# Batch 0's head loads on SyncE, its folds in quarters, and an earlier softmax in a cross-covariance attention with FFN kernel

## Chip, cores and metric

One core of a Trainium2 chip. The metric is the device time of one execution in microseconds (us), smaller is better. The span of a profiled execution is about 2 us shorter than its time.

## The reference

```python
def _attn_ref(q, k, v, tau):                       # B, N, C = 4, 5824, 256
    qn = q / (norm(q, axis=1) + 1e-6)
    kn = k / (norm(k, axis=1) + 1e-6)
    s = kn.transpose(0, 2, 1) @ qn / tau           # 256 x 256 per batch
    a = exp(s - s.max(-1)); a /= a.sum(-1) + 1e-9
    return v @ a

def _moe_ref(x, w1, w2, w3, w_out):                # x: 23296 x 256, d_ff 1024
    return ((x @ w1) * (x @ w2)) @ w3 @ w_out
```

## The kernel before

The kernel folds each batch's 256x256 attention matrix into the weights w1 and w2 (`Wf`), and w3 with w_out into one matrix (`W_sb`). Then the main loop needs only v, transposed: 11 chunks of 512 rows and a short one per batch, and per chunk eight steps `j`, each with two products `a`, `b` (2 matmuls of 512 columns each), one multiplication and up to two groups of output matmuls `o`. While batch b runs in this loop, the scores of batch b+1 (`G`, from q and k) and its softmax and folds are put in between, at set values of a clock that counts the planned TensorE time from the first `a` of the batch. I call the place where the softmax and folds of the next batch meet the end of this one a joint; there are three.

What the argument needs:

```python
    load_piece("k", 0, 0, (half,))      # GpSimd, f32 -> bf16 in the transfer
    load_piece("q", 0, 0, (half,))
    ...
        def first_folds():              # batch 0, before the first `a`
            sum_mm(0)
            fold_mm(0, 0)
            fold_mm(1, 0)
            sum_mm(1)
            fold_mm(0, 1)
            fold_mm(1, 1)
            fold(2)
            transpose_half_on_pe(0, 0, 0, False)
            fold(3, on_act=True)
            fold(4, "out", on_act=False)
            fold(5, "out")
    ...
            + [(0.2, 15.5, sums)]                                             # batches 1 to 3
            + [(0.43, 16.5 + 0.85 * i, lambda i=i: fold(i)) for i in range(8)]
    ...
    def hold(src):                      # GpSimd stands until src has been written
        nc.gpsimd.tensor_copy(gate_t, src)
    ...
        if b == 0:
            for i in range(2):
                at(1.5 + 0.6 * i, 0.43, soft0[5 + i])
            ...
            moves = [("v", 0, 3, 29.0), ("qk", 1, 0, 38.0), ("qk", 1, 1, 43.0), ("v", 0, 4, 50.0), ("qk", 1, 2, 58.0)]
            moves += [("qk", 1, 3, 63.0), ("v", 0, 5, 70.0), ("qk", 1, 4, 81.0), ("qk", 1, 5, 87.0)]
            moves += [("v", 1, 0, 96.0), ("v", 1, 1, 106.0), ("v", 1, 2, 116.0), ("qk", 2, 0, 126.0)]
            t0, t1 = 57.0, 115.5        # the scores of batch 1 are spread over this clock time
        ...
        before = (0, 2) if b == 0 else None
        for nm, m, pi, t in moves:
            if before is not None:      # the load that follows a load of v waits for v's DMA transpose
                at(t, 0.0, lambda w=before: hold(...vTs of piece w...))
            at(t, 0.0, gate)
            if nm == "qk":
                at(t, 0.0, lambda m=m, pi=pi: load_qk(m, pi))
                before = None
            else:
                at(t, 0.0, lambda m=m, pi=pi: load_piece("v", m, pi))
                at(t + 4.0, 0.0, lambda m=m, pi=pi: transpose_piece(m, pi))   # SyncE, DMA transpose
                before = (m, pi)
```

Each name in `moves` stands for a load of one piece (8 of 45 row tiles). All loads go out from GpSimd, one after the other, so a `hold` stops every load behind it. `gate` is of the same kind: it lets GpSimd stand until the loop's latest product has been made, so that a load goes out no sooner than its place on the clock.

## Time and profile before

| | before |
|---|---|
| time, median (six runs beside the changed kernel) | 573.24 us (572.98 to 575.30) |
| span of the profiled execution | 571.7 us |
| TensorE busy | 559.4 us, 98% |
| first `a` of the main loop | 40.69 us |
| chain that ended last | TensorE 92%, DMA 5% |

TensorE is the bound: before 40.69 us it waits for q and k of batch 0, after it it hardly rests. The lines stand in the prediction. To see small losses I kept one account for every run: for a stretch of the trace, the time from the first matmul start in it to the first start after it, less the matmuls in between, each with N/2400 + 0.0026 us for N columns (0.216 us at 512 and 0.109 at 256, the two rates that the steady stretch shows). What is left is TensorE time lost to waits and to a lower clock. Single matmul records are missing from some traces; each missing record of a fold reads as 0.22 us of loss and is taken off. By it the kernel before loses 1.02, 0.67 and 1.55 us at its three joints (168 to 192, 290 to 320, 424 to 454 us), 0.77 in the last chunk, and under 0.1 us in any stretch between them. The expectations of the experiments were written with a coarser count, up to 0.4 us off; the numbers in the text are the exact ones.

### The profile page before, as it was taken

The page shows a single profiled execution, that of the slowest core. Times are in us where ns is not written, and L with a number is a line of the kernel's source. Part 1 is how long each engine was busy: PE and PEld are TensorE (multiplying, and loading weights), DVE is VectorE, ACT ScalarE, POOL GpSimd, SP SyncE. Part 2 cuts the span into 40 slices and gives each one's busy share as a digit, 9 for nine tenths or more (in the row PEclk, how much of TensorE's full clock was granted, in tenths as well). Part 3 has the DMA queues.
Part 4 walks back from the last instruction along what each step waited for, and adds up shares of the span by engine and source line. Part 5 has one row for each costly group of instructions (what it writes and reads, how often), then busy time and mean ns, then how long its engine had stood idle before and what let it go on. Part 6 is the DMA issues. An engine that isn't in the chain of part 4 may idle for free.

```text
span 571.7 us, 10102 instructions
## 1 busy us (share of the span) xinstructions
PE 559.4 (98%) x3750; PEld 354.5 (62%) x3750; DVE 377.4 (66%) x612; ACT 337.7 (59%) x624; POOL 83.3 (15%) x164
## 2 busy tenths in 40 slices
PE   7789999999999999999999999999999999999997
PEld 4655576776666666666666666666665666666665
DVE  1047744788977567887776667778876656565564
ACT  0046644777856567776766567767766554454453
POOL 5250020303030111121030012031120000000000
PEclk9999999999999999999999999999999999999999
DMA  8999959869685697495661595665640325221011
GB/s 163 211 187 208 184 104 240 170 149 242 140 183 118 123 204 150 94 192 121 145 144 72 99 215 123 140 136 126 175 110 38 85 73 148 63 63 75 38 72 58
DMA packets 74560, 76.93 MB, mean 135 GB/s; under 512 B 54160, under 2 KB 58256, under 8 KB 74512
## 3 DMA queue, kind: packets, MB, share of 16 engines
q0 software_dynamic: 15504, 39.46, 39.3%
q1 hardware_dynamic: 58784, 36.64, 22.2%
q8 instruction: 29, 0.48, 0.3%
q10 hardware_dynamic: 224, 0.20, 0.1%
q14 instruction: 19, 0.16, 0.1%
HBM read 78.91 MB, written 23.86 MB: 180 GB/s over the span
## 4 chain that ended last, share of the span: by engine, by line
PE 92%; DMA 5%; DVE 1%; ACT 1%; POOL 1%; issue 0%; ACTq 0%; POOLq 0%
PE o L479 28%; PE a L438 27%; PE b L438 27%; PE G L188 5%; DMA k<-in_k_dram 5%; PE fold L349 2%; PE w L596 1%; ACT as L444 0%; ACT kr L279 0%; POOL k L109 0%; POOL q L109 0%; DVE abs L453 0%; PE sqk L221 0%; DVE vT L136 0%; DVE abs L455 0%
## 5 line engine op out<-in xcount | busy, mean ns | idle before, releaser
L453 DVE TENSOR_TENSOR abs<-as,b 128x512 bf16<-128x512 bf16 x336 | 230.5, 687 | 141.4 <-ACT as L444 130.3
L444 ACT CAST as<-a 128x512 bf16<-128x512 f32 (+1 forms) x384 | 216.1, 563 | 176.9 <-DVE abs L453 90.2
L438 PEld LDWEIGHTS <-Wf 128*128 128x128 bf16 x1536 | 149.2, 98 | 102.0 <-issue 1.9
L479 PE MATMUL o<-W_sb,abs 128*128 128x256 bf16 x1376 | 209.6, 273 | 0.1
L438 PE MATMUL a<-vT,Wf 128*128 128x512 bf16 x704 | 209.4, 379 | 0.2
L438 PE MATMUL b<-vT,Wf 128*128 128x512 bf16 x704 | 209.3, 379 | 0.0
L479 PEld LDWEIGHTS <-abs 128*128 128x128 bf16 x1376 | 134.5, 98 | 81.6 <-DVE abs L455 0.3
L197 DVE TENSOR_TENSOR acc<-acc,sq 128x1024 f32<-128x1024 f32 x66 | 80.4, 1219 | 0.4 <-ACT sq L185 0.3
L188 PE MATMUL G<-k,q 128*128 128x256 bf16 x276 | 49.9, 273 | 0.0
L185 ACT ACTIVATE sq<-q 128x512 f32<-128x512 bf16 x66 | 41.8, 634 | 0.0
L185 ACT ACTIVATE sq<-k 128x512 f32<-128x512 bf16 x66 | 41.6, 630 | 0.0
L426 POOL COPY gate_t<-abs 1x1 bf16<-1x1 bf16 x39 | 13.9, 355 | 167.7 <-DVE abs L453 167.0
L500 DVE COPY osb<-o 128x512 f32<-128x512 f32 x44 | 30.1, 685 | 0.7 <-PE o L479 0.7
L430 POOL COPY gate_t<-vT 1x1 bf16<-1x1 bf16 x17 | 4.4, 258 | 169.3 <-DMA vT<-v 134.0
L188 PEld LDWEIGHTS <-q 128*128 128x128 bf16 x276 | 27.0, 98 | 3.1
L499 ACT COPY osb<-o 128x512 f32<-128x512 f32 x44 | 25.8, 586 | 3.8 <-PE o L479 1.8
L279 ACT ACTIVATE kr<-row 128x256 f32<-128x256 f32 x1 | 0.4, 385 | 31.6 <-PE row L267 31.6
L109 POOL DMA_DIRECT2D q<-in_q_dram x29 | 15.7, 541 | 13.2 <-DMA k<-in_k_dram 6.0
L349 PE MATMUL fold<-w,e 128*128 128x512 bf16 x64 | 17.0, 380 | 0.5 <-DVE vT L136 0.4
L356 ACT ACTIVATE Wf<-fold,rs 128x512 bf16<-128x512 f32 x16 | 10.9, 688 | 8.1 <-PE fold L349 6.4
L244 DVE TENSOR_TENSOR dk<-sqk,ident 128x256 f32<-128x256 f32 x1 | 0.4, 425 | 21.3 <-PE sqk L221 21.3
L109 POOL DMA_DIRECT2D k<-in_k_dram x25 | 13.8, 551 | 3.7 <-DMA k<-in_k_dram 1.9
(89 smaller groups left out, 240.4 us busy)
## 6 DMA issues: line engine op xcount, KB each, us to landing
out_dram<-osb SPq DMA_DIRECT2D x44, 512.0 KB, 3.1
k<-in_k_dram POOLq DMA_DIRECT2D x19, 512.0 KB, 8.5
v<-in_v_dram POOLq DMA_DIRECT2D x19, 512.0 KB, 5.2
q<-in_q_dram POOLq DMA_DIRECT2D x18, 512.0 KB, 6.6
w_wout<-in_moe_w_dram POOLq DMA_DIRECT2D x1, 2048.0 KB, 23.6
k<-in_k_dram POOLq DMA_DIRECT2D x4, 320.0 KB, 9.9
v<-in_v_dram POOLq DMA_DIRECT2D x4, 320.0 KB, 5.4
q<-in_q_dram POOLq DMA_DIRECT2D x4, 256.0 KB, 12.0
```

The costliest lines, as they stand in the source:

```text
L109: nc.gpsimd.dma_start(out=pieces[nm, n, pi][:, lo:hi, :], in_=qk_main[nm, n][0][:, pi * PIECE + lo : pi * PIECE + hi, :])
L185: nc.scalar.activation(out=dst[:, :, part, :], in_=src[:, o : o + 2, :], func=AF.Square)
L188: nc.tensor.matmul(G[:, ct, :], lhsT=qt[:, i, ct * P : (ct + 1) * P], rhs=kt[:, i, :], start=(pr == 0 and part == 0 and ct == 0), stop=(pr ...
L197: nc.vector.tensor_add(accs[n], accs[n], sqs[0])
L349: nc.tensor.matmul(st["fold", i], lhsT=st["e"][:, c2, c1 * P : (c1 + 1) * P], rhs=w12[:, c2, w, h * 512 : (h + 1) * 512], start=(c2 == 0), ...
L426: nc.gpsimd.tensor_copy(gate_t, last_ab[0][:1, :1])
L438: nc.tensor.matmul(t[:, :n], lhsT=Wf[b][:, ct, w, j * P : (j + 1) * P], rhs=rhs_of(b, c, ct), start=(ct == 0), stop=(ct == CT - 1),)
L444: nc.scalar.copy(a_sb[:, :n], tiles[0][:, :n])
L453: nc.vector.tensor_mul(ab, a_sb, tiles[1])
L479: nc.tensor.matmul(tl[h][:, o, :], lhsT=lhsT, rhs=W_sb[:, j, :], start=(j == 0 and o == 0), stop=(j == FT - 1 and (small or o == 1)), skip ...
L499: nc.scalar.copy(o[:, 0:2, :], tl[0])
L500: nc.vector.tensor_copy(o[:, 2:4, :], tl[1])
```

## The change

The intent is in four parts. (1) The first halves of q and k of batch 0 come from SyncE in f32, sooner than GpSimd starts, and are cast. (2) Only the first quarter of the folded weights is made before the first `a`, the rest after it. (3) In batch 0, q and k of batch 1 are loaded ahead of late pieces of v, and the scores of batch 1 start at clock 46, not 57. (4) The later softmaxes start up to 4 us sooner, and every other fold goes to the bank `G` of the products. The core of the diff:

```diff
         def first_folds():
             sum_mm(0)
-            fold_mm(0, 0)
-            fold_mm(1, 0)
+            for c1 in range(CT):
+                quarter_mm(0, c1, 0)
             sum_mm(1)
-            fold_mm(0, 1)
-            fold_mm(1, 1)
-            fold(2)
-            transpose_half_on_pe(0, 0, 0, False)
-            ...
+            for c1 in range(CT):
+                quarter_mm(0, c1, 1)
+        def second_quarter():
+            ...
-            + [(0.2, 15.5, sums)]
-            + [(0.43, 16.5 + 0.85 * i, lambda i=i: fold(i)) for i in range(8)]
+            + [(0.2, 16.5, sums)]
+            + [(0.43, 17.8 + 0.9 * i, lambda i=i: fold(i, "G" if i % 2 else "ab")) for i in range(8)]
...
-    load_piece("k", 0, 0, (half,))
-    load_piece("q", 0, 0, (half,))
+    for nm in "kq":
+        new_piece(nm, 0, 0)
+        raw[nm] = work.tile([P, half, C], F32, tag="o_sb", name=f"raw_{nm}", bufs=3)
+        nc.sync.dma_start(out=raw[nm], in_=qk_main[nm, 0][0][:, :half, :])
+        load_part(nm, 0, 0, half, PIECE)
...
+    nc.vector.tensor_copy(pieces["k", 0, 0][:, :half, :], raw["k"])
+    nc.scalar.copy(pieces["q", 0, 0][:, :half, :], raw["q"])
...
-    for h in range(2):            # w1, w2 by halves of 512 columns
+    for f0, f1 in ((0, 256), (256, 512), (512, F)):
...
-            for i in range(2):
-                at(1.5 + 0.6 * i, 0.43, soft0[5 + i])
+            at(0.5, 0.87, soft0[5])
+            for i in range(4):
+                at(2.3 + 0.6 * i, 0.43, soft0[6 + i])
...
-            moves = [("v", 0, 3, 29.0), ("qk", 1, 0, 38.0), ("qk", 1, 1, 43.0), ("v", 0, 4, 50.0), ("qk", 1, 2, 58.0)]
-            moves += [("qk", 1, 3, 63.0), ("v", 0, 5, 70.0), ("qk", 1, 4, 81.0), ("qk", 1, 5, 87.0)]
-            moves += [("v", 1, 0, 96.0), ("v", 1, 1, 106.0), ("v", 1, 2, 116.0), ("qk", 2, 0, 126.0)]
-            t0, t1 = 57.0, 115.5
+            moves = [("qk", 1, 0, 29.0), ("v", 0, 3, 30.0), ("qk", 1, 1, 43.0), ("qk", 1, 2, 47.0), ("v", 0, 4, 53.0)]
+            moves += [("qk", 1, 3, 62.0), ("qk", 1, 4, 66.0), ("v", 0, 5, 72.0), ("qk", 1, 5, 81.0)]
+            moves += [("v", 1, 0, 94.0), ("v", 1, 1, 104.0), ("v", 1, 2, 114.0), ("qk", 2, 0, 126.0)]
+            t0, t1 = 46.0, 104.0
         else:
             ...
-            t0, t1 = 16.0, 104.0
+            t0, t1 = 16.0, 99.0
```

More of the change, by code (lines that the diff above doesn't have):

```diff
@@ L340, in sums, with fold_mm @@
             sum_mm(1)
-        def fold_mm(i, c2, tag="ab", on_act=None):
-            h, rest = divmod(i, 4)
-            w, c1 = divmod(rest, 2)
+        def fold_mm(key, c2, tag="ab", on_act=True):
+            w, c1, lo, hi = key
             if c2 == 0:
-                st["fold", i] = psum.tile(
-                    [P, 512], F32, tag=tag, name=f"fold_{n}_{i}", bufs={"ab": 4, "out": 3}[tag]
+                st[key] = psum.tile(
+                    [P, 512], F32, tag=tag, name=f"fold_{n}_{w}_{c1}_{lo}", bufs={"ab": 4, "out": 3, "G": 1}[tag]
                 )
+            m = st[key][:, : hi - lo]
             nc.tensor.matmul(
-                st["fold", i], lhsT=st["e"][:, c2, c1 * P : (c1 + 1) * P], rhs=w12[:, c2, w, h * 512 : (h + 1) * 512],
+                m, lhsT=st["e"][:, c2, c1 * P : (c1 + 1) * P], rhs=w12[:, c2, w, lo:hi],
                 start=(c2 == 0), stop=(c2 == CT - 1),
@@ L353, in fold_mm @@
             if c2 == CT - 1:
-                dst = Wf[n][:, c1, w, h * 512 : (h + 1) * 512]
-                if on_act if on_act is not None else i % 2 == 0:
-                    nc.scalar.activation(out=dst, in_=st["fold", i], func=AF.Copy, scale=st["rs"][:, c1 : c1 + 1])
-                else:
-                    nc.vector.tensor_scalar_mul(dst, st["fold", i], st["rs"][:, c1 : c1 + 1])
-        def fold(i, tag="ab", on_act=None):
-            fold_mm(i, 0, tag)
-            fold_mm(i, 1, tag, i % 2 == 0 if on_act is None else on_act)
+                dst = Wf[n][:, c1, w, lo:hi]
@@ new lines, in fold_mm, with fold, quarter_mm @@
+                if on_act:
+                    nc.scalar.activation(out=dst, in_=m, func=AF.Copy, scale=st["rs"][:, c1 : c1 + 1])
+                else:
+                    nc.vector.tensor_scalar_mul(dst, m, st["rs"][:, c1 : c1 + 1])
+        def fold(i, tag="ab"):
+            h, rest = divmod(i, 4)
+            w, c1 = divmod(rest, 2)
+            for c2 in range(CT):
+                fold_mm((w, c1, h * 512, (h + 1) * 512), c2, tag, i % 2 == 0)
+        def quarter_mm(lo, c1, c2):
+            if c2 == 0:
+                tag = "ab" if lo == 0 else "out"
+                st[lo, c1] = psum.tile(
+                    [P, 2, 256], F32, tag=tag, name=f"quarter_{lo}_{c1}", bufs={"ab": 4, "out": 3}[tag]
+                )
+            m = st[lo, c1]
+            for w in range(2):
+                nc.tensor.matmul(
+                    m[:, w, :], lhsT=st["e"][:, c2, c1 * P : (c1 + 1) * P], rhs=w12[:, c2, w, lo : lo + 256],
+                    start=(c2 == 0 and w == 0), stop=(c2 == CT - 1 and w == 1), skip_group_check=True,
+                )
+            if c2 == CT - 1:
+                for o in (0, P) if lo == 0 else (slice(0, 256),):
+                    cols = slice(o, o + P) if lo == 0 else o
+                    dst, src = Wf[n][:, c1, :, lo : lo + 256][:, :, cols], m[:, :, cols]
+                    if c1 == 0:
+                        nc.scalar.activation(out=dst, in_=src, func=AF.Copy, scale=st["rs"][:, c1 : c1 + 1])
+                    else:
+                        nc.vector.tensor_scalar_mul(dst, src, st["rs"][:, c1 : c1 + 1])
@@ L364, in first_folds @@
         def first_folds():
             sum_mm(0)
-            fold_mm(0, 0)
-            fold_mm(1, 0)
+            for c1 in range(CT):
+                quarter_mm(0, c1, 0)
             sum_mm(1)
-            fold_mm(0, 1)
-            fold_mm(1, 1)
-            fold(2)
-            transpose_half_on_pe(0, 0, 0, False)
-            fold(3, on_act=True)
-            fold(4, "out", on_act=False)
-            fold(5, "out")
+            for c1 in range(CT):
+                quarter_mm(0, c1, 1)
@@ L377, in soft_units @@
+        def second_quarter():
+            for c1 in range(CT):
+                for c2 in range(CT):
+                    quarter_mm(256, c1, c2)
         if n == 0:
-            return [k_first, k_row, q_first, scaled_first, first_folds] + [lambda i=i: fold(i) for i in range(6, 8)]
+            return [k_first, k_row, q_first, scaled_first, first_folds, second_quarter] + [lambda i=i: fold(i) for i in range(4, 8)]
         return (
@@ L511 @@
     half = PIECE // 2
-    busy(14)
-    load_piece("k", 0, 0, (half,))
-    load_piece("q", 0, 0, (half,))
+    busy(10)
+    raw = {}
+    for nm in "kq":
[3 more added lines that the diff above has]
+        load_part(nm, 0, 0, half, PIECE)
     w3_wout = vT_pool.tile([P, (NT - 1) * C], BF16, tag="vT", name="w3_wout")
@@ L561 @@
     load_piece("q", 0, 5, (1, 3, 4))
-    for h in range(2):
-        hs = slice(h * F // 2, (h + 1) * F // 2)
-        nc.gpsimd.dma_start(out=w12[:, :, 0, hs], in_=w1r[:, :, hs])
-        nc.gpsimd.dma_start(out=w12[:, :, 1, hs], in_=w2r[:, :, hs])
-        if h == 0:
-            new_piece("v", 0, 0)
-        load_part("v", 0, 0, h * half, (h + 1) * half)
+    new_piece("v", 0, 0)
+    load_part("v", 0, 0, 0, half)
+    for f0, f1 in ((0, 256), (256, 512), (512, F)):
+        nc.gpsimd.dma_start(out=w12[:, :, 0, f0:f1], in_=w1r[:, :, f0:f1])
+        nc.gpsimd.dma_start(out=w12[:, :, 1, f0:f1], in_=w2r[:, :, f0:f1])
+    load_part("v", 0, 0, half, PIECE)
     load_piece("v", 0, 1)
@@ L588 @@
     soft0[3]()
-    busy(4)
+    busy(3)
+    transpose_half_on_pe(0, 0, 0, False)
     soft0[4]()
```

## The prediction

> **What bounds the kernel now.** I read the page first, then the chain of waits, then the timeline from 0 to 82 us, then busy time in short windows at the start and at the three places where one batch's softmax meets the next batch.
>
> From the page, its first part and its share of the chain that ended last:
>
> ```profile
> PE 559.4 (98%) x3750; PEld 354.5 (62%) x3750; DVE 377.4 (66%) x612; ACT 337.7 (59%) x624; POOL 83.3 (15%) x164
> PE 92%; DMA 5%; DVE 1%; ACT 1%; POOL 1%; issue 0%; ACTq 0%; POOLq 0%
> ```
>
> TensorE is the bound, and DMA has 5% of the chain. In the chain in order of time that share is two pieces at the start:
>
> ```profile
> 4.52 11.89 DMA k<-in_k_dram
> 16.69 14.79 DMA k<-in_k_dram
> 31.53 0.84 PE sqk L221 x12
> ...
> 39.07 0.70 DVE vT L136
> 39.82 1.04 PE fold L349 x4
> 40.85 0.43 PE a L438 x2
> ```
>
> Columns are start, length, what. Until 31.5 us the kernel waits for k and q of batch 0; then come softmax and folding, and the first product `a` of the main loop. The timeline has that product's start at 40.69. From there until 567.72 (end of the last matmul) TensorE hardly rests. To see how hardly, I counted matmuls by shape. In the ab-only stretch (57.57 to 63.62) seven steps of four 512-column matmuls take 6.05 us, so 0.216 us each, and a 256-column one 0.109 (four with L479 fill the 1.300 us step: (1.300-0.864)/4). By these rates the matmuls after 40.69 need about 523.3 us, of 527.0. Some 3.7 us are lost: about 0.9 around 168-190 us, 0.5 around 296-318, 1.5 around 428-450, 0.8 in the last chunk. The last is untouched by the change. So the whole change plays for the 40.7 us before the loop and for under 3 us inside it.
>
> The very start, windows of 0.5 us (length; then PE, PEld, DVE, ACT, POOL busy; clock, DMA share, GB/s):
>
> ```profile
> 2.00:2.50 0.50, 0.50 (x3) 0.16 (x2) 0.00 (x0) 0.01 (x1) 0.50 (x2) 1.00 0.00 0
> 2.50:3.00 0.50, 0.50 (x3) 0.22 (x2) 0.00 (x0) 0.00 (x0) 0.50 (x2) 1.00 1.13 53
> 3.00:3.50 0.50, 0.50 (x3) 0.22 (x2) 0.00 (x0) 0.00 (x0) 0.50 (x2) 1.00 0.49 66
> 3.50:4.00 0.50, 0.50 (x3) 0.15 (x1) 0.00 (x0) 0.00 (x0) 0.50 (x3) 1.00 1.00 184
> 4.00:4.50 0.50, 0.50 (x2) 0.15 (x1) 0.00 (x0) 0.00 (x0) 0.50 (x2) 1.00 1.16 209
> ```
>
> The DMA engines do nothing before 2.5 us, full rate comes at about 3.5, and from there to 31 us they run at 205 to 225 GB/s (counted on the bf16 side) without a gap. That stream is the bound of the head, so what starts it sooner ends it sooner.
>
> **What the Trainium skill says.** "DMA: Bandwidth & Descriptors", section "Latency and other measured facts", gives a first byte after about 0.6 us for DMAs issued from SyncE or ScalarE and about 1 us for those of GpSimd. The trace has GpSimd's first issue at 1.22 and the first DMA activity at 2.5, so 1.3 us here; no SyncE load stands in it to compare. The same page, "Queues, rings and completion order", says that each DMA engine takes turns between the queues that have work: so SyncE's two loads will share the engines with GpSimd's from 2.5 us on, and the total is what counts. "TensorE: Matmul & The Clock Gate", section "Back-to-back issue gap", gives N/2.4 + 2.5 ns for an isolated warm matmul, 215.8 ns at 512 columns; the trace agrees (216). "PSUM — Partial Sum Buffer", section "Specifications (TRN2)", counts 8 banks; the kernel's pools take 4 (ab), 3 (out) and 1 (G), all 8, which is why folds can only borrow.
>
> **The change part by part.**
>
> *First halves of q and k by SyncE in f32, then cast.* No bytes of HBM are saved; the stream starts sooner. SyncE is released as the other engines are (the first DVE work is at 0.80). I take its issue at 0.8 to 1.0 and data at full rate from about 2.4 instead of 3.5; in 2.5 to 3.5 the engines moved only 60 of 209 GB/s, so part of that hole is filled. Estimate 1.0 us, between 0.5 and 1.5. The casts (128x1024) are new: 0.7 to 1.2 us on DVE by what its 1024-element copies and adds take (687, 1219 ns), 1.0 on ACT (the 128x1024 copy of vT took 1.01). Both engines are idle then (ACT until 33.6), and the first squares, now at 6.24 us, do not set the end: TensorE waits again for pieces at 11, 14 and 20 us. Four warm-up matmuls fewer cost and save nothing. After 24.8 us TensorE waited only 0.4 us, but its work is released by these landings, so it moves with them.
>
> *Quarters first.* Before, between the exponentials (37.37) and 40.69 stand 10 of 12 fold matmuls, a transpose of v with its 0.70 us evacuation, and a wait for w; the timeline shows both gaps:
>
> ```profile
> 38.87 0.59 PE L349 MATMUL fold<-w,e 128*128 128x512 bf16 x2
> 39.82 1.04 PE L349 MATMUL fold<-w,e 128*128 128x512 bf16 x4 [0.35 <-DVE vT L136]
> 40.69 0.59 PE L438 MATMUL a<-vT,Wf 128*128 128x512 bf16 x2
> ```
>
> After, only eight 256-column matmuls (0.87 us) come first, four before the last exponential lands; they end near 38.05. The row sums' reciprocal is ready near 38.1 as now, then one 256-element evacuation on ACT and DVE each (0.42, from 0.40 for such shapes and 0.69 to 0.75 for 512). First `a` near 38.75: 1.94 us sooner. But more is owed after it: before, two folds (0.87 us); now the second quarter (0.87) and four folds (1.73), 2.60 in all. Net 1.94 - 1.73 = 0.2 us. TensorE idles about 0.7 us there for the evacuation, where it idled about 0.9. The transpose moves into the idle time before the exponentials; its v is now loaded ahead of the weights and should land near 34.6 (w's first load did, issued at 30.0 and 4.6 us later), before TensorE reaches it at about 35.7.
>
> *Order of loads in batch 0 and earlier scores.* Same bytes, same matmuls. Scores of batch 1 move from clock 57-115 to 46-104, into the stretch in which output matmuls are caught up, where a step has 1.73 us of TensorE for one DVE multiplication. It removes the meeting of folds with the short last chunk (around 175-182).
>
> *Later softmax sooner, folds by turns in G.* The same 16 matmuls per batch. By the instruction order, all folds now end before chunk 11; previously they ran into it in all three batches. Two of three folds in a group no longer take ab banks together. Against it: in each batch two folds in the single G bank follow with only one other fold (0.43 us) between them, and need an evacuation of 0.75 on DVE: up to 0.5 us of stall. The exponentials' ping-pong (ACT waits 1.09 us for DVE, four times in batches 2 and 3) stays. Of about 2.9 us lost at these places I expect 0.5 back, between -0.5 and 1.5.
>
> Sum: 1.0 + 0.2 + 0.5 = 1.7 us, so 571.4. As each part shifts work that had slack rather than adding any, I lean a little further: 571.2.
>
> **Rivals.**
> 1. *The DMA start gives nothing*: two f32 writes of 0.5 MB share the engines and cost more than bf16 ones, or the quarters' 512-byte rows slow the weights (single-token loads around 31 to 33 us went at 135 to 153 GB/s). For it: DMA share is already above 1. Against: all reads are f32 anyway. Then only 0.7 us remain: 572.4.
> 2. *A wait for W's own transposes takes its place.* The w3T transposes are issued at 59.85, when w3 has landed, take 4.4 us, and were needed at 67.07: a slack of 2.8 us. The need comes 1.94 us sooner relative to the DMA stream, so about 0.9 remains. A slower weight load would use it up: at worst 1 us, 572.2.
> 3. *Early scores wait for q and k.* Piece 1 of batch 1 waits for v3's transpose; I get its landing near 92 and its need near 94. If late, TensorE stops for 1 to 3 us: up to 574.
> 4. *The full prize*: the stream starts 1.5 us sooner and the batch joints lose only half of what they did: 1.5 + 0.2 + 1.5, 569.9.
>
> **Range and chances.** The parts' spread gives 569.3 to 572.9. 2% is 11.5 us. Faster by that would need more than all idle time inside the loop plus a head shortened by a fifth: 1 in 100. Slower by that would need a stall that no view suggests.
>
> **What would show it.** DMA activity before 2.5 us and the last k landing near 30.5 show step one; first `a` near 37.7 step two (it should move by more than the end does); first w matmul near 64, unwaited; no TensorE loss around batch 1's joint, and small stalls at folds in G. The prediction is wrong if the head gains over 3 us, if TensorE waits at batch 1's first scores, or if the joints get worse by more than they were.

## The result, and the profile after

The changed kernel took 579.12 us (median of six runs, 578.51 to 579.30) against 573.24 us: 1.0094 of the time before, 95% interval 1.0079 to 1.0109. That is within the 2% of "same", but it is 5.9 us slower where 2.0 us faster was predicted, and outside the range. Ratios here are the mean time of one kernel's fast runs over that of the other's in the same rounds, so not quite the ratio of the medians. Executions over 1.5% slower than the fastest of the same kernel are left out of the means.

The page of the kernel after, its first part and the chain's shares:

```profile
PE 560.5 (97%) x3746; PEld 356.5 (62%) x3753; DVE 379.1 (66%) x614; ACT 338.3 (59%) x626; POOL 85.4 (15%) x164
PE 77%; DMA 10%; issue 7%; POOL 2%; ACT 2%; DVE 1%; POOLq 0%; ACTq 0%
```

TensorE fell from 92% to 77% of the chain and DMA rose from 5% to 10%: a transfer now stands in the path inside the loop. What TensorE waited for in the kernel after, by line and releaser (total us, times, longest):

```profile
PE G L188 <- DMA k<-in_k_dram: 3.2, 1, 3.2
PE fold L350 <- DVE Wf L359: 1.4, 3, 0.5
PE b L463 <- DVE Wf L359: 0.8, 1, 0.8
PE a L463 <- DVE Wf L387: 0.6, 1, 0.6
```

The first three of these waits are not in the kernel before: its score matmuls waited for nothing. (`L188` are the scores, `L350` the folds, `L463` the products `a` and `b`.) The timeline of TensorE in the kernel after shows where the largest is:

```profile
114.70 0.60 PE L504 MATMUL o<-W_sb,abs 128*128 128x256 bf16 x4
118.54 0.38 PE L188 MATMUL G<-k,q 128*128 128x256 bf16 x2 [3.25 <-DMA k<-in_k_dram]
```

It is the first product of piece 3 of batch 1. Windows of 5 us of the kernel after (length; PE, PEld, DVE, ACT, POOL busy; granted clock, DMA share, GB/s):

```profile
110.00:115.00 5.00, 5.00 (x38) 3.52 (x37) 3.25 (x4) 3.80 (x7) 5.00 (x9) 1.00 0.89 202
115.00:120.00 5.00, 1.75 (x14) 1.23 (x13) 2.43 (x3) 1.51 (x4) 0.24 (x1) 0.98 1.05 211
120.00:125.00 5.00, 5.00 (x28) 3.11 (x27) 2.62 (x5) 2.62 (x6) 0.00 (x0) 0.68 0.95 183
```

The last window in the kernel before:

```profile
120.00:125.00 5.00, 5.00 (x38) 3.46 (x36) 3.52 (x5) 3.93 (x8) 0.00 (x0) 1.00 0.47 88
```

After the wait TensorE is busy all the time, but at 0.68 of its clock in the mean: 28 matmuls where the kernel before did 38. So the wait costs more than itself. The account by stretch, in us:

| | before | after | difference |
|---|---|---|---|
| first `a` | 40.69 | 37.54 | -3.15 |
| fold matmuls still owed then | 0.87 | 2.60 | +1.73 |
| lost, first `a` to 66 us | 0.0 | 1.0 | +1.0 |
| lost, 66 to 112 | 0.0 | 0.2 | +0.2 |
| lost, 112 to 130 | 0.0 | 5.1 | +5.1 |
| lost, 130 to 168 | 0.0 | 0.3 | +0.3 |
| lost, three joints | 3.2 | 3.5 | +0.3 |
| after the last matmul | 3.8 | 3.7 | -0.1 |

For the four fold records that the trace of the kernel after lacks (52 of 56, one in the head and one at each joint), 0.22 us is taken off its first row of losses and off each of its joints. The rows sum to +5.4 us, as much as the span grew (571.66 to 577.04).

At the start, windows of 0.5 us of the kernel after show the first step of the change at work:

```profile
1.50:2.00 0.50, 0.50 (x2) 0.15 (x1) 0.28 (x1) 0.50 (x1) 0.50 (x2) 1.00 0.79 90
2.50:3.00 0.50, 0.50 (x3) 0.23 (x2) 0.00 (x0) 0.00 (x0) 0.50 (x2) 1.00 0.69 197
```

The DMA engines are at work before 2.0 us, where the kernel before had nothing until 2.5. (The GB/s count SyncE's loads in f32, so they are not to be compared with the bf16 figures of before.) The last piece of k lands at 15.97 + 14.56 = 30.53 us by the chain, against 31.48 before: 0.95 us sooner.

**Why piece 3 was late.** GpSimd's timeline in the kernel after, where all the loads are issued (L109) and the holds stand (L455):

```profile
88.22 0.53 POOL L109 DMA_DIRECT2D q<-in_q_dram  x1
...
89.90 0.54 POOL L109 DMA_DIRECT2D k<-in_k_dram  x1
...
93.81 0.53 POOL L109 DMA_DIRECT2D v<-in_v_dram  x1
109.50 0.18 POOL L455 COPY gate_t<-vT 1x1 bf16<-1x1 bf16 x1 [15.16 <-DMA vT<-v]
...
111.26 0.54 POOL L109 DMA_DIRECT2D k<-in_k_dram  x1
```

and in the kernel before:

```profile
92.19 0.53 POOL L109 DMA_DIRECT2D v<-in_v_dram  x1 [0.27 <-issue]
105.42 0.60 POOL L430 COPY gate_t<-vT 1x1 bf16<-1x1 bf16 x1 [12.71 <-DMA vT<-v]
...
108.46 0.54 POOL L109 DMA_DIRECT2D k<-in_k_dram  x1
```

In the kernel after, v's piece 4 is issued behind pieces 1 and 2 of q and k, its transpose is issued at 105.71, and the hold for that transpose passes at 109.50. Only then go q and k of piece 3. k's piece lands 7.24 us after its issue, at 118.5. TensorE is ready for it at 115.3. In the kernel before, the same piece was issued 2.8 us sooner, at 108.46, took 12.4 us to land, at 120.82, and its first product started at 129.20, with no wait:

```profile
129.20 0.60 PE L188 MATMUL G<-k,q 128*128 128x256 bf16 x4
```

The change asks for the data 14 us sooner and gets it 2.3 us sooner.

### The profile page after: what moved, and what is told of

The parts are those of the page before. It is cut to its first block, busy times and chain, and to the rows that moved or that the text cites. A ratio compares the mean times of both kernels' runs of the same rounds, so it can differ in the third digit from the quotient of the medians.

```text
span 577.0 us, 10120 instructions
## 1 busy us (share of the span) xinstructions
PE 560.5 (97%) x3746; PEld 356.5 (62%) x3753; DVE 379.1 (66%) x614; ACT 338.3 (59%) x626; POOL 85.4 (15%) x164
## 4 chain that ended last, share of the span: by engine, by line
PE 77%; DMA 10%; issue 7%; POOL 2%; ACT 2%; DVE 1%; POOLq 0%; ACTq 0%
PE o L504 24%; PE a L463 23%; PE b L463 23%; DMA k<-in_k_dram 7%; PE G L188 5%; DMA v<-in_v_dram 2%; PE fold L350 1%; ACT as L469 1%; DVE abs L478 1%; DMA vT<-v 1%; DMA out_dram<-osb 1%; POOL q L109 0%; POOL w L597 0%; DVE Wf L359 0%; POOL k L109 0%
## 5 line engine op out<-in xcount | busy, mean ns | idle before, releaser
L463 PEld LDWEIGHTS <-Wf 128*128 128x128 bf16 x1536 | 149.2, 98 | 102.7 <-issue 1.9
L463 PE MATMUL b<-vT,Wf 128*128 128x512 bf16 x704 | 210.0, 380 | 0.8 <-DVE Wf L359 0.8
L463 PE MATMUL a<-vT,Wf 128*128 128x512 bf16 x704 | 209.6, 379 | 0.8 <-DVE Wf L387 0.6
L188 PE MATMUL G<-k,q 128*128 128x256 bf16 x276 | 50.5, 274 | 3.3 <-DMA k<-in_k_dram 3.2
L451 POOL COPY gate_t<-abs 1x1 bf16<-1x1 bf16 x39 | 16.5, 424 | 175.9 <-DVE abs L478 174.9
L188 PEld LDWEIGHTS <-q 128*128 128x128 bf16 x276 | 27.1, 98 | 6.8 <-issue 2.6
L455 POOL COPY gate_t<-vT 1x1 bf16<-1x1 bf16 x17 | 4.9, 288 | 178.2 <-DMA vT<-v 168.8
L109 POOL DMA_DIRECT2D q<-in_q_dram x28 | 15.1, 539 | 12.5 <-DMA k<-in_k_dram 5.4
L350 PE MATMUL fold<-w,e 128*128 128x512 bf16 x52 | 14.0, 379 | 1.6 <-DVE Wf L359 1.4
L478 DVE TENSOR_TENSOR abq<-as,b 128x512 bf16<-128x512 bf16 x16 | 10.9, 686 | 5.4 <-ACT as L469 4.8
L357 ACT ACTIVATE Wf<-fold,rs 128x512 bf16<-128x512 f32 x14 | 9.6, 687 | 8.2 <-PE fold L350 6.9
L109 POOL DMA_DIRECT2D k<-in_k_dram x24 | 13.5, 562 | 4.2 <-DMA k<-in_k_dram 3.4
```

Source lines behind the costliest of these rows:

```text
L109: nc.gpsimd.dma_start(out=pieces[nm, n, pi][:, lo:hi, :], in_=qk_main[nm, n][0][:, pi * PIECE + lo : pi * PIECE + hi, :])
L188: nc.tensor.matmul(G[:, ct, :], lhsT=qt[:, i, ct * P : (ct + 1) * P], rhs=kt[:, i, :], start=(pr == 0 and part == 0 and ct == 0), stop=(pr ...
L350: nc.tensor.matmul(m, lhsT=st["e"][:, c2, c1 * P : (c1 + 1) * P], rhs=w12[:, c2, w, lo:hi], start=(c2 == 0), stop=(c2 == CT - 1),)
L451: nc.gpsimd.tensor_copy(gate_t, last_ab[0][:1, :1])
L463: nc.tensor.matmul(t[:, :n], lhsT=Wf[b][:, ct, w, j * P : (j + 1) * P], rhs=rhs_of(b, c, ct), start=(ct == 0), stop=(ct == CT - 1),)
L478: nc.vector.tensor_mul(ab, a_sb, tiles[1])
```

## The experiments

All were correct. Each edit is against the kernel named. Theory at the outset: the late k piece 3 costs most of it, the eighth fold and the G bank some tenths each. Rival: the head (the SyncE loads, the quarters) or the joints cost it.

**1. scores_late** (after, with batch 1's scores at the old clock):

```diff
-            t0, t1 = 46.0, 104.0
+            t0, t1 = 57.0, 115.5
```

> The changed kernel with batch 1's scores back at clock 57 to 115.5; loads keep the new order. Theory (early scores meet a k that lands late): piece 3 is then needed about 11 us later, near 126, and k still lands near 118.5, so the 3.25 us wait of TensorE and the slow clock after it (5.1 us together) vanish: 574.0, within 0.7. Rival (the new order of loads costs by itself, through DMA traffic or a late v): it stays near 579.

Measured: 574.80 us, 1.0025 [1.0013, 1.0037] of before. No wait of the scores is left, and 4.3 us of the 5.9 are gone. The early scores are the main cause. But 1.7 us of loss remain where the prediction had a gain. The early scores did serve their purpose in part: the first joint loses 1.0 us in the kernel after and 1.9 here.

**2. moves_before** (after, early scores, with the list of loads of before):

```diff
-            moves = [("qk", 1, 0, 29.0), ("v", 0, 3, 30.0), ("qk", 1, 1, 43.0), ("qk", 1, 2, 47.0), ("v", 0, 4, 53.0)]
+            moves = [("v", 0, 3, 29.0), ("qk", 1, 0, 38.0), ("qk", 1, 1, 43.0), ("v", 0, 4, 50.0), ("qk", 1, 2, 58.0)]
             (and the two lines after it)
```

> The changed kernel with batch 0's loads in the old order and times, scores early (46 to 104). Theory: the old order never was meant for early scores: k piece 4 was issued at 128 before and would be issued near 125 to 128, landing near 133, while it is needed near 125: a wait of about 8 us there, and 582 to 588 in all. Rival (order of loads at fault, not the early scores): the wait goes and the time is 574.

Measured: 596.86 us, 1.041 [1.0396, 1.0425]. The line of the waits:

```profile
PE G L188 <- DMA k<-in_k_dram: 15.9, 3, 6.8
```

Pieces 0, 2 and 4 of k were late, where I had expected piece 4 alone, and the time lies 9 us above my range. So the new order of loads is a help to the early scores; it does not go far enough.

**3. no_hold** (after, without the hold before q and k piece 3):

```diff
-            if before is not None:
+            if before is not None and (nm, m, pi) != ("qk", 1, 3):
```

> The changed kernel, but the load of q and k piece 3 of batch 1 no longer waits for v piece 4's transpose (the hold on it; the check for races passes). Theory: GpSimd then issues the pair near 100 instead of 110.7, k lands near 108, before it is needed at 115.3: no wait there, 574 unless a later piece is late in turn (piece 4 follows at once, piece 5 waits for v5). Rival (DMA bandwidth, not the hold, is what makes k late): issue earlier, landing still after 115, a wait of 1 us or more stays.

Measured: 594.36 us, the median of the four fast runs (589.25 to 595.52; two more at 599.88 and 600.55), 1.0346 [1.0308, 1.0385]. My expectation was wrong by 20 us, though its first half came true: k's piece 3 was issued at 104.34, landed at 112.15 and was not waited for (first product at 116.29). The loss came from elsewhere. From the issue of a transpose of v to the landing of vT it took, in the kernel after (60 to 150 us) and in this one (100 to 145 us, two transposes):

```profile
DMA to landing us min/median/max: 2.7/3.7/4.3
```

```profile
DMA to landing us min/median/max: 2.7/17.5/32.2
```

With loads in flight the transpose of v's piece 4 took 32.2 us, not 3.7, the loads of q and k piece 4 beside it took 28.4 and 30.4, and DMA moved 69 to 106 GB/s in the five windows of 5 us from 110 to 135, where the kernel after has 183 to 211 from 110 to 125. Output transfers came out late (ScalarE waited 15.8 us for one), output tiles ran out, and TensorE waited 15.3 us:

```profile
130.00:135.00 5.00, 0.00 (x0) 0.00 (x0) 0.00 (x0) 0.00 (x0) 0.00 (x0) 0.64 0.92 69
```

The hold is therefore no needless caution: it keeps loads away from a transpose. The remedy can't be to drop it.

**4. head_only** (after, with the load order, the score times and the later softmax of before; only the SyncE loads and the quarters remain):

```diff
-            + [(0.2, 16.5, sums)]
-            + [(0.43, 17.8 + 0.9 * i, lambda i=i: fold(i, "G" if i % 2 else "ab")) for i in range(8)]
+            + [(0.2, 15.5, sums)]
+            + [(0.43, 16.5 + 0.85 * i, lambda i=i: fold(i)) for i in range(8)]
             (moves as in moves_before)
-            t0, t1 = 46.0, 104.0
+            t0, t1 = 57.0, 115.5
-            t0, t1 = 16.0, 99.0
+            t0, t1 = 16.0, 104.0
```

> The kernel before with the new start alone (SyncE's first loads, quarters, order of weights and v), old plan of loads, scores and softmax. By the two traces: first product 3.15 us sooner, 1.73 us more of fold work owed after it, 1.2 to 1.5 us lost at the fold that the fifth step waits for: net 0 to -0.3, so 572.9 to 573.3. If the 1.5 us are caused by something else of the change (early scores, loads), 571.7.

Measured: 575.90 us, 1.0052 [1.0034, 1.0069]; a miss by 2.8 us. The head lost 2.0 us after the first `a` (37.78), and k of batch 1 (piece 4) was 1.2 us late at 130 to 150 us although its clock was the old one. The reason: the clock counts from the first `a`, so a sooner first `a` pulls every later need forward with it, while the chain of loads, transposes and holds moved much less (this piece landed at 138.76, and at 138.89 in the kernel before).

**5. sp_only** (before, with the SyncE loads and casts alone):

```diff
-    busy(14)
-    load_piece("k", 0, 0, (half,))
-    load_piece("q", 0, 0, (half,))
+    busy(10)
+    (the SyncE loads and the two casts, as in the change)
```

> The kernel before with SyncE's f32 first halves and their casts alone. If the stream's earlier start is the whole of it: k's last piece lands 0.95 us sooner (as it did in the changed kernel), first product near 39.8, all later waits shift with it: 572.2, within 0.4. Rival (the casts or the f32 writes cost what the start gains): 573.1.

Measured: 572.49 us, 0.9986 [0.9973, 0.9998]. First `a` at 39.33, 1.36 us sooner than in the trace of before, and the time 0.8 us shorter. Not all of the 1.36 is SyncE's: the same head has its first `a` at 39.70, 39.79 and 39.40 in experiments 12, 16 and 17, and the head of before has it at 40.34 in experiment 15, so by the means it is about 1.0. There is a new wait of 0.5 us for k at batch 1's scores. The load chain had next to nothing to spare there: in the kernel before, k's piece 4 lands at 138.89 and its first product starts at 139.19.

**6. quarters_only** (head_only without the SyncE loads):

```diff
-    busy(10)
-    (the SyncE loads and the two casts)
+    busy(14)
+    load_piece("k", 0, 0, (half,))
+    load_piece("q", 0, 0, (half,))
```

> The kernel before with quarters, the order of v and weights, and the moved transpose, without SyncE's loads. First product near 38.5 (3.15 less 0.95 us sooner), 1.73 us more owed, 1.2 to 1.5 us lost at the fifth step's fold: 573.6 to 574.2 by that alone. The weights in quarters fall behind by about 1 us in the DMA stream (the new start alone moved 106 to 132 GB/s in 34 to 38 us where the kernel before moved 160 to 178), so the waits for w3T and for a late k that the new start alone had (0.3 and 1.2 us) should show again: up to 575.5. If it comes to 573.0 or less, the loss sits in SyncE's loads.

Measured: 577.38 us, 1.0068 [1.0055, 1.008]. First `a` at 38.39, then a loss of 1.1 us in the head and 1.6 at batch 1's scores, where k was 1.5 us late. The profiled execution was itself the fastest of this kernel, 576.53, and its losses beyond those of before are 1.1 in the head, 1.6 at the scores and 0.6 at the joints; with 1.7 owed and less 2.3 by the sooner `a` that makes 2.8, as much as its span is longer. Why the other runs took about 1 us more stays open. Of the two changes to the head the quarters are the one that loses.

**7. late_fold7** (scores_late, and the four late folds of batch 0 placed 0.5 apart instead of 0.6):

```diff
-                at(2.3 + 0.6 * i, 0.43, soft0[6 + i])
+                at(2.3 + 0.5 * i, 0.43, soft0[6 + i])
```

> As scores_late, but the last four folds of batch 0 at steps of 0.5 instead of 0.6 of the clock, which puts the eighth fold before the fourth step, as in the kernel before. Theory (the fifth step's b waits 0.85 us for this fold's evacuation, and a slow ACT behind it): that wait goes, 0.8 to 1.4 us less than scores_late's 574.8: 573.4 to 574.0. Rival (the four folds in a row hold all ab banks and the wait only moves): 574.8.

Measured: 574.05 us, 1.0009 [0.9998, 1.0021], so 0.75 less than scores_late. It was run at another time. It tests the wait of 0.85 us that the timeline of the kernel after shows before a `b`:

```profile
45.70 0.39 PE L463 MATMUL b<-vT,Wf 128*128 128x512 bf16 x1 [0.85 <-DVE Wf L359]
```

The eighth fold makes columns that the fifth step is the first to read. Placed 0.6 apart, it stands directly before that step, and its evacuation queues on VectorE behind the copy of a transposed v:

```profile
44.31 0.68 DVE L136 COPY vT<-tr_I-588_589 128x1024 bf16<-128x1024 bf16 x1
44.91 0.74 DVE L359 TENSOR_SCALAR Wf<-fold,rs 128x512 bf16<-128x512 f32 x1
```

One step sooner, the wait is gone, and the loss in the head falls from 1.0 (scores_late) to 0.45: part of the time is lost at smaller waits instead.

**8. scores_mid** (after):

```diff
-            t0, t1 = 46.0, 104.0
+            t0, t1 = 51.0, 109.0
```

> The changed kernel with batch 1's scores at clock 51 to 109, 5 us later than in the change. k piece 3 is then needed near 120 and lands near 118.5: no wait there, so 574.0 (579.1 less 5.1), also less than scores_late's 574.8 if the early softmax of batch 1 is worth anything. If the stall had another cause than this one late piece, it comes back at piece 4 or 5 and the time is over 576.

Measured: 575.41 us, 1.0034 [1.0018, 1.0051]. k's piece 3 was in time, but piece 5 was still 1.2 us late, and an output tile 0.7. Five us later is not enough.

**9. no_g** (late_fold7, all folds in the bank group ab):

```diff
-            + [(0.43, 17.8 + 0.9 * i, lambda i=i: fold(i, "G" if i % 2 else "ab")) for i in range(8)]
+            + [(0.43, 17.8 + 0.9 * i, lambda i=i: fold(i)) for i in range(8)]
```

> As late_fold7, but all folds of batches 1 to 3 in the ab banks, at the same clock. late_fold7's trace has three waits of TensorE for the evacuation of a fold in G, 1.4 us together. Theory (folds by turns in G cost these waits): they go and 0.7 to 1.4 us with them: 572.7 to 573.4. Rival (with all in ab the wait only moves to the next step's a or b, as in the kernel before): 574.0.

Measured: 573.22 us, 0.9992 [0.9969, 1.0014], 0.8 us less than late_fold7, the same but for G, took, and 0.8 less than halves_w, which has G and other weight loads. The three waits of 0.5 us for the bank, one in each joint, are gone, and the joints lose 3.1 us where late_fold7's lose 4.5. That the time gains less has a reason in the trace: the head of this profiled run lost 1.3 us, not 0.45, at waits for w (0.3) and for the transposed w3 (0.4).

**10. halves_w** (late_fold7, w1 and w2 loaded by halves as before):

```diff
-    for f0, f1 in ((0, 256), (256, 512), (512, F)):
+    for f0, f1 in ((0, 512), (512, F)):
```

> As late_fold7, but w1 and w2 loaded in two halves each behind v, not in two quarters and a half. Theory (four small loads with rows of half the length lower the DMA rate in 34 to 40 us to 128 to 178 GB/s): the rate there rises to about 160 to 200, w3 lands near 59.2 instead of 59.9, the first quarter's weights still come in time or cost under 0.5 us. The time itself hardly changes in this kernel, since nothing waits for w3: 573.6 to 574.1. Rival (the rate falls because GpSimd's eight open loads are smaller whatever their rows, or by something else): rate and w3 stay.

Measured: 574.05 us, 1.0016 [0.9991, 1.0041], no better than late_fold7. But the windows of 2 us in which the weights load differ. The kernel after, then this one (the last two columns are DMA share and GB/s):

```profile
34.00:36.00 2.00, 1.18 (x14) 0.79 (x13) 1.73 (x9) 1.50 (x6) 2.00 (x5) 1.00 1.13 123
36.00:38.00 2.00, 1.44 (x15) 0.87 (x12) 1.35 (x5) 1.01 (x3) 1.88 (x3) 1.00 1.10 147
38.00:40.00 2.00, 2.00 (x15) 1.32 (x14) 1.20 (x2) 1.36 (x3) 0.28 (x1) 1.00 1.09 165
```

```profile
34.00:36.00 2.00, 1.12 (x11) 0.64 (x10) 1.73 (x8) 1.08 (x5) 2.00 (x4) 1.00 1.22 181
36.00:38.00 2.00, 1.31 (x12) 0.79 (x12) 1.14 (x5) 0.85 (x3) 0.84 (x2) 1.00 1.10 155
38.00:40.00 2.00, 1.62 (x11) 1.09 (x12) 1.10 (x3) 1.38 (x4) 0.00 (x0) 1.00 1.18 210
```

With rows of 256 bf16 elements (512 bytes) the engines are nearly as busy (1.11 against 1.17 in the mean) and move about a fifth less. late_fold7, which differs from this kernel in these loads alone, has 131, 143 and 178 GB/s. Each of the loads is also half as large, so whether it is the row or the size of a load is not separated. The end of the stream, w3's landing, shows in the first issue of w3's transposes: 59.85 us before, 59.15 in sp_only, 59.95 after, 59.06 here, 60.17 in quarters_only. So the quarter loads give back nearly all of the 0.95 us that SyncE won. In this kernel's time it does not show: nothing waits for w3, and the first `a` comes 0.8 us later than in late_fold7 (38.38), as TensorE's quarters wait for larger pieces of w until 36.8.

**11. old_joints** (halves_w, with the later softmax of before):

```diff
-            + [(0.2, 16.5, sums)]
-            + [(0.43, 17.8 + 0.9 * i, lambda i=i: fold(i, "G" if i % 2 else "ab")) for i in range(8)]
+            + [(0.2, 15.5, sums)]
+            + [(0.43, 16.5 + 0.85 * i, lambda i=i: fold(i)) for i in range(8)]
-            t0, t1 = 16.0, 99.0
+            t0, t1 = 16.0, 104.0
```

> As halves_w, with the softmax timing, the fold timing and the ab banks of the kernel before: only the new start and the new order of loads in batch 0 are left, the eighth fold early. By the traces' accounts the joints of late_fold7 lose 0.5 to 1.0 us more than those of before: 573.1, within 0.4, so the same as before. If it goes under 572.5 the new start is worth more than SyncE's loads alone (572.5).

Measured: 573.15 us, 1.0000 [0.9977, 1.0024]: 0.9 less than halves_w beside it. Of the new joints nothing is a gain so far.

**12. sp_late** (sp_only):

```diff
-            t0, t1 = 57.0, 115.5
+            t0, t1 = 60.0, 118.5
```

> As sp_only, with batch 1's scores 3 us later (60 to 118.5). sp_only's trace has one new wait, 0.5 us for a late k of batch 1 that the earlier start brought up: it goes, 572.0 to 572.2. If the joint behind it gets worse by the later softmax, 572.5 to 573.

Measured: 573.23 us, 0.9997 [0.9977, 1.0017]. The wait for k is gone as expected, but the first joint loses 1.3 us where sp_only's loses 1.0, which may be the later scores pressing on the softmax. The rest of the difference is not the edit's: the first `a` came 0.37 us later than in sp_only's trace, and the other two joints, which the edit does not touch, lost 0.4 more. Executions differ by as much, so that the slack is merely moved from one side to the other is not shown.

**13. v4_first** (after, v's piece 4 ahead of q and k piece 2, to get its transpose over sooner):

```diff
-... ("qk", 1, 1, 43.0), ("qk", 1, 2, 47.0), ("v", 0, 4, 53.0)]
+... ("qk", 1, 1, 43.0), ("v", 0, 4, 44.0), ("qk", 1, 2, 48.5)]
```

> The changed kernel with one load moved: v piece 4 ahead of q and k piece 2 of batch 1, which now waits for v4's transpose. Theory (k piece 3 is late because v4 lands behind two pairs of q and k, and its transpose holds the pair): v4 lands near 97, its transpose near 101, k piece 2 near 108, k piece 3 near 113. So TensorE's wait for piece 3 at 115 goes, but piece 2, needed near 105, comes about 2 us late: a wait of 1.5 to 3 us there and 576 to 577.5 in all. Rival (the DMA engines have no room for these loads at all in this stretch): k piece 3 lands after 116 as before and both waits stand: 580 or more.

Measured: 583.68 us (580.30 to 584.65), 1.0162 [1.0138, 1.0186].

```profile
113.68 0.58 PE L188 MATMUL G<-k,q 128*128 128x256 bf16 x2 [7.58 <-DMA k<-in_k_dram]
```

Piece 2, behind the hold, was late: the hold passed at 104.87 where I had worked out 101. The wait moved and grew. Piece 3 was in time only because TensorE had stood before: it landed at 118.61, no sooner than in the kernel after (118.50), as the rival had said. Piece 1 was 0.85 us late as well.

**14. v4_first_50** (v4_first, without the two other faults that were known by then):

```diff
-            + [(0.43, 17.8 + 0.9 * i, lambda i=i: fold(i, "G" if i % 2 else "ab")) for i in range(8)]
+            + [(0.43, 17.8 + 0.9 * i, lambda i=i: fold(i)) for i in range(8)]
-                at(2.3 + 0.6 * i, 0.43, soft0[6 + i])
+                at(2.3 + 0.5 * i, 0.43, soft0[6 + i])
-            t0, t1 = 46.0, 104.0
+            t0, t1 = 50.0, 108.0
```

> v4_first with the scores at 50 to 108, the eighth fold early, and all later folds in ab. Piece 2 is then needed near 108.5, as it lands, pieces 3 to 5 later than they land: no wait over 0.5 us at the scores, batch 1's joint early and without G: 572.3 to 573.2, no better than SyncE's loads alone (572.5) if the joints keep their exponentials' waits. If it goes under 572, early scores are worth something once the loads keep up.

Measured: 575.91 us, 1.0052 [1.004, 1.0065]: one wait of 2.9 us for k's piece 2, and 4.7 us lost around it (96 to 130 us). No order that I tried brings q and k in time for scores much before clock 57.

**15. joints_only** (before, with the later softmax of the change):

```diff
-            + [(0.2, 15.5, sums)]
-            + [(0.43, 16.5 + 0.85 * i, lambda i=i: fold(i)) for i in range(8)]
+            + [(0.2, 16.5, sums)]
+            + [(0.43, 17.8 + 0.9 * i, lambda i=i: fold(i, "G" if i % 2 else "ab")) for i in range(8)]
-            t0, t1 = 16.0, 104.0
+            t0, t1 = 16.0, 99.0
```

> The kernel before with the change's later softmax alone: scores of batches 2 and 3 end 5 us sooner, folds later and by turns in G; batch 1's scores stay. By the traces, G costs up to 0.5 us per batch and the third joint gains: 573.1 to 573.9. If the change's own idea of the joints holds, 572.5.

Measured: 574.72 us, 1.0027 [1.0004, 1.005].

```profile
PE fold L349 <- DVE Wf L358: 2.1, 5, 0.5
```

Five waits for the single bank, none over 0.5 us, 2.1 us together, and 1.7 us more time, 0.8 above my range.

**16. sp_joints** (sp_only, with the later softmax of the change but for G):

```diff
-            + [(0.2, 15.5, sums)]
-            + [(0.43, 16.5 + 0.85 * i, lambda i=i: fold(i)) for i in range(8)]
+            + [(0.2, 16.5, sums)]
+            + [(0.43, 17.8 + 0.9 * i, lambda i=i: fold(i)) for i in range(8)]
-            t0, t1 = 57.0, 115.5
+            t0, t1 = 58.0, 113.0
-            t0, t1 = 16.0, 104.0
+            t0, t1 = 16.0, 99.0
```

> sp_only with the change's softmax timing for batches 2 and 3, all folds in ab, and batch 1's scores at 58 to 113. v4_first_50's trace lost 0.5, 0.7 and 0.7 us at the three joints so timed without G, the kernel before 1.0, 0.5 and 1.3; sp_only has 572.5: so 571.6 to 572.2, faster than both kernels. If the joints' losses depend on where the short chunk falls and not on G, 572.5.

Measured: 575.34 us, spread from 571.97 to 578.11, 1.0029 [0.9993, 1.0065]. Scores that are squeezed into less time meet a late k again (3.5 us in the profiled run). The second and third joints, though, lose only 0.58 and 0.78, against 0.67 and 1.55 in the kernel before.

**17. sp_joints_23** (sp_only, with the new softmax times, without G, only where the loads have slack):

```diff
-            + [(0.2, 15.5, sums)]
-            + [(0.43, 16.5 + 0.85 * i, lambda i=i: fold(i)) for i in range(8)]
+            + [(0.2, 15.5 if n == 1 else 16.5, sums)]
+            + [(0.43, 16.5 + 0.85 * i if n == 1 else 17.8 + 0.9 * i, lambda i=i: fold(i)) for i in range(8)]
...
-            t0, t1 = 16.0, 104.0          # batches 1 to 3
+            t0, t1 = 16.0, 99.0
```

> SyncE's loads, batch 0's plan and batch 1's softmax as in sp_only; the later softmax timing for batches 2 and 3 alone, folds in ab. sp_joints' trace lost 0.2 and 0.5 us at those joints, sp_only's 0.6 and 1.2, and sp_joints' late k came from ending batch 1's scores earlier, which is undone here: 572.5 less 1.1, 571.2 to 571.8, ratio near 0.997. If it is 572.5, the joints' accounts in the traces do not carry over to the time.

Measured: 572.08 us (571.65 to 572.15), 0.998 [0.9966, 0.9993] of before: faster than both kernels, by 0.2% of the one before, and 0.3 us above my range. The joints lose 1.02, 0.74 and 0.67; only the third gains.

## Why the prediction was wrong

**The start on SyncE: right, then given back.** Predicted 1.0 us, measured 0.95 at k's last landing. "Rivals" 1 was half true as well: the quarter loads slowed the weights, and w3 landed no sooner than before (experiment 10). The start alone is worth 0.8 us of time (experiment 5).

**First `a` near 37.7: right, 37.54.** The 1.73 us owed after it were right too. What the step left out was where the late folds land among the steps. The eighth stands in the step that reads it, and 0.85 us of waiting follow (experiment 7). The net gain of 0.2 us of this part became a loss of about 0.5 us in the head (2.2 sooner without SyncE's share, 1.7 owed, 1.0 lost; quarters_only says 0.6).

**The failed step.** It stands in the prediction as "Same bytes, same matmuls. Scores of batch 1 move from clock 57-115 to 46-104, into the stretch in which output matmuls are caught up". It priced TensorE's work and not the landing of what the work reads. The third rival did name a wait of the scores for q and k, but it looked at piece 1 only, gave it 2 us of slack (landing near 92, need near 94), and stopped. Even there the slack was not real: piece 1 landed at 95.97 and its first product started at 96.02, 0.2 us late by the account. That it cost no more was luck; in no_hold, with the same plan up to there, it came 1.3 us late. Piece 3 stands behind a hold as well, the one for v's piece 4. The numbers for it lay in the trace of before: from v's issue to the end of its hold 13.2 us (92.19 to 105.42), from k's issue to its landing 8.5 (the median on the page). In the new order v's piece 4 comes at clock 53, so at 37.7 + 53 = 90.7 at the soonest; 13.2, about 1.5 for the gate and q's issue, and 8.5 make a landing at 113.9. The need: the scores are 69 units (three for each of 23 pairs of row tiles), and piece 3 starts with the 37th; spread over the 58 us from clock 46 that is 46 + 30.3 = 76.3, at 114.0. That estimate has no slack at all; in the event v's load went out at 93.81, 3 us later, and the hold took 15.7 us from it. What the runs showed in place of that step: k's piece 3 landed at 118.50, TensorE was ready at 115.30, and the wait with the slow clock behind it cost 5.1 of the 5.9 us; with the scores back at clock 57, 4.3 us are gone. The landing hardly moves with the plan: it is at 117.9 to 121.0 in 16 of the 19 traces, later in two (sp_late, moves_before), and sooner (112.15) only without the hold. Experiments 1, 8 and 14 show the cost falling with the lateness of the scores, 2 and 13 show it growing with the lateness of the loads.

**The price of a wait.** The 3.25 us wait cost about 5.1. The rival's "1 to 3 us" would have been too small even with the right piece, as the granted clock was halved afterwards. The Trainium skill says it in "TensorE: Matmul & The Clock Gate", section "What's actually happening": after an idle window of about 3.4 us the clock is halved until the engine has been busy for as long, and the window runs free of the kernel. The traces agree: when the clock falls, it falls to 0.50, for 3.41 us or a multiple of it, and 3.25 + 3.41/2 makes 5.0. Two such windows of the kernel after, and two of sp_joints:

```profile
116.41:119.82 3.41, 1.28 (x10) 0.97 (x10) 0.92 (x2) 1.01 (x3) 0.00 (x0) 1.00 1.06 214
119.82:123.24 3.42, 3.42 (x14) 1.98 (x13) 2.09 (x3) 1.48 (x3) 0.00 (x0) 0.50 1.07 207
```

```profile
135.42:138.83 3.41, 1.87 (x14) 1.15 (x12) 2.21 (x3) 1.32 (x3) 1.51 (x2) 1.00 0.99 198
138.83:142.24 3.41, 1.46 (x10) 0.92 (x10) 0.00 (x0) 1.02 (x2) 0.00 (x0) 1.00 1.11 242
```

In the kernel after, 2.1 us of one window were idle, and the next ran at 0.50. In sp_joints the wait was longer, 3.49 us, but lay across two windows (1.5 and 2.0 us idle): the clock stayed at 1.00, and the wait cost 3.6. In v4_first_50 a wait of only 2.9 us lay within one window; the next ran at 0.50, and 4.7 us were lost. In v4_first, with 7.6 us of wait, the clock was at 0.50 from 108.34 to 118.58, and 10.1 us were lost. So in these traces a wait's price depends on where it falls among the windows, which the plan does not set.

**Joints: predicted +0.5, measured about -0.3.** "Up to 0.5 us of stall" for the folds in G was the right size for each one: three of them, 1.4 us. What was wrong was to book the gain beside it. Without G and without squeezing batch 1 the earlier softmax may gain 0.4 us against sp_only (572.08 and 572.49, the same chip); the intervals, 0.9966 to 0.9993 and 0.9973 to 0.9998 of before, do not separate the two.

**Range and chances.** The change stayed within 2%, as the prediction held all but certain. The range of 569.3 to 572.9 did not hold; it was made from the spread of the parts (which at their best, 1.5 + 0.2 + 1.5, give 569.9 and not 569.3) and had left the named stall of up to 574 outside. To "lean a little further", as each part shifted work that had slack, was the same error as the failed step: the slack of the transfers had not been worked out.

**What stays open.** The 0.3 us that the kernel after loses between 130 and 168 us are not traced. About 1 us of quarters_only's time lies outside its profiled losses. Differences under 1 us between calls rest on different chips, and single traces of one and the same head differ by up to 0.5 us.

## What to carry to other kernels

When work is moved sooner, work out for each transfer that it reads when it lands and when it is needed, piece by piece, along the queue that issues them; it is the pieces behind a forced wait that are late, and not only the first of them. A schedule counted from its own first instruction moves all its needs forward when the head gets shorter, while transfers stay where their queue puts them: a shorter head needs slack in the loads behind it. And fold or evacuate through a single bank only if more than one evacuation's time lies between two uses.

## What the Trainium skill lacked or had wrong

- "DMA: Bandwidth & Descriptors", "Rules for kernel authors", says that a transpose next to ordinary DMAs needs nothing. That speaks of right results, and the results were right; the time is missing. In no_hold one transpose took 32.2 us from issue to landing beside loads, against 3.7 us in the median of the kernel after, which keeps them apart; the loads took 28 to 30 us, and the rate fell to 69 to 106 GB/s. Only this one overlap was profiled; all six runs of the kernel were at 589 us or more.
- The same page's "Specifications" give 512 bytes as enough for line rate. While loads that wrote rows of exactly 512 bytes were under way the engines moved 123 to 165 GB/s, and 155 to 210 with rows of 1024, at nearly the same busy share. As each load was also half as large, this does not prove the page wrong.
- "TensorE: Matmul & The Clock Gate", "What's actually happening", gives an idle window of about 3.4 us, and the traces agree. What it does not say is how much of a window must be idle: 2.1 of 3.41 us were enough in the kernel after, 2.0 in sp_joints were not, so a wait of 2.9 us halved the clock and one of 3.49 us did not.
- For the first byte of a SyncE load, "DMA: Bandwidth & Descriptors", "Latency and other measured facts", gives about 0.6 us. In the kernel after the issue runs from 0.73 to 1.13 us, and the first packet of SyncE's queue starts at 1.75: 0.6 us from the issue's end, 1.0 from its start.
